# A fused attention and token-mixing kernel: the first four x tiles turned on TensorE in place of DMA transposes, with new engine orders

## The chip, the cores and the metric

The kernel runs on one core of a Trainium2 chip. The metric is device time in microseconds of one execution. The kernel before was timed three times: median 170.32 us, lowest 170.24, highest 170.61. One further execution was profiled; everything said about single instructions comes from that one.

## The reference, cut to what matters

```python
x = A_x                                        # (1, 2048, 448), bf16
g = sigmoid((x * gate_w).sum(-1, keepdims=True))
# A: 16 heads of 28, four segments of 512 rows
q, k, v = x @ wq, x @ wk, x @ wv               # split by head and segment
for s in range(4):
    a_dot = softmax(q_s @ k_s.T * 28**-0.5 + causal_mask) @ v_s
    a_mem = (phi(q_s) @ M) / (phi(q_s) @ z + 1e-6)
    o_s = sigmoid(beta) * a_mem + (1 - sigmoid(beta)) * a_dot
    M, z = M + phi(k_s).T @ v_s, z + phi(k_s).sum(rows)
a = concat(o) @ wo
# B: mixing over the 2048 rows (tokens), per column of x
h = layernorm(x)
u = gelu(h.T @ w1 + b1)                        # (448, 1792)
b = (u @ w2 + b2).T
out = g * a + (1 - g) * b
```

## The kernel before, in words

x has 2048 rows, held as 16 tiles of 128 rows. It is needed in two layouts. As rows (`xh`, one slot for each tile) it feeds the layer norm and then the first mixing product. Turned (`xT`, feature on the partition, the 448 features cut into four chunks c that start at 0, 128, 256 and 320) it feeds the projections to v, k and q. The kernel loads x twice: as rows by plain DMAs (`load_x`, names `ldx0`, `ldx4` and so on, after the first tile of each), and turned by DMA transposes (`transpose_x`, names `dtx{tc}_0` for chunks 0 to 2 and `dtx{tc}_1` for chunk 3, where tc counts groups of four tiles, 512 rows).

The program is a list of operations with names. Each states what it reads and writes, and the semaphore waits are worked out from that. The order on each engine is not decided by a scheduler at run time: it is written out in the table `ORDER`, one list of names for each of TensorE (PE), ScalarE (ACT), VectorE (DVE), GpSimd (POOL) and SyncE (SP). A number behind `@` is the PSUM bank that the operation takes, a number behind `*` a repeat.

Names that the rest of this document uses:

- `warm`, `warm2`: products of constants into bank 3 that nothing reads; `gtr`: a product that turns the gate weights, behind the load `ldgw`; `gw`: their copy by DVE into the weights of v.
- `pra{t}`, `prb{t}`, `lo{t}`, `prt{t}`: the v projection of tile t, by chunks 0, 1, the shared last 128 rows of the features, and the rest. `prk`, `prx`, `prq` with `lok`, `loq`: the same for k and q of a group and a set of heads.
- `ldwv*`, `ldwk*`, `ldwq*`: weight loads. ACT issues those of v and one of k, SP the others. `ldb1`, `ldb2`: biases, issued by ACT. `padk*`, `padx*`, `padq*`: copies by DVE that spread the weights of k and q to 32 columns for each head.
- `cpv`, `cpk`, `cpq`: copies from PSUM after a projection (ACT or DVE); `gt`: the gate's tanh on ACT; `ek`, `eq`: exponentials for phi.
- `bns`, `bna`, `ln`: layer norm statistics and application, on DVE. `sc`: scores; `exp`: softmax exponentials on ACT, 2048 columns each; `mask`: causal masks on POOL; `pv`: probabilities times v; `ot`: the turn of the attention output on DVE; `lw`, `wo`: output projection; `u`, `y`: the two mixing products; `ag`: gating of the attention output; `fin` and `out`: last mix and store.

TensorE runs products in several shapes: over the whole array, over two halves of its rows (`lo*`), over four strips of 32 rows (`sc`) or of 32 columns (`pv`, and `u`, `y` products that stand beside a `pv`). Products of one line (L296) appear for nearly all projections and mixing products, since one helper issues them.

The start of the program, in order: ACT issues the loads of the v weights and the gate weights; SP issues the DMA transposes of the first group (`dtx0_0`, `dtx0_1`), then the weights of k and q, then the transposes of the second group, then rows of x; TensorE runs nine `warm` products, `gtr`, `warm2`, and then the v projections of tiles 0 to 3. `early` projections (group 0) take banks 0 to 3 in turn.

The lines that the change touches: `transpose_x(0)` with the loads below it (from line 552), `warm_up` (line 660), the resources of `xT` (line 500: two for each group, chunks 0 to 2 and chunk 3), their use in `proj_d`, `do_k` and `do_v` (lines 761 to 870), and `ORDER` (line 318).

Of the kernel before, what the change touches and what calls it, by code (L numbers as in the profile page):

```python
# [324 lines left out]
u1-15 u2-10*4 u3-5*2 u4-0@4 u3-7*2 sc1_1 u5-0@6*2 u2-14 u5-2*2 u2-15 u3-9*6 u5-4 u3-15 u4-1*5 u5-5*2 pv1@7 u4-6*2
sc1_2 u4-8 u5-7*5 u4-9*4 u5-12 pv0@5 u5-13 sc1_3 u4-13*3 u6-0@7*3 u7-0@5 u6-3 u5-14 u6-4*2 u5-15 u6-6 sc1_4 u6-7 u7-1
u6-8*4 u7-2*2 u6-12 u7-4*3 u6-13*3 sc2_0 u7-7*7 pv2@6 u7-14*2 sc2_1 mst0@4 u8-0@6*2 prq2_1@7 prq2_0@5 loq2_0 sc2_2
u8-2*4 prq2_2@4 u8-6*4 prq2_2h@7 loq2_2 mem1 u8-10*2 u9-0@4 u8-12 u9-1*8 u8-13*2 u11-0@5 sc2_3 u9-9*3 pv3@7 u9-12
u8-15 u9-13*2 u11-1 u9-15 u11-2*4 sc2_4 u10-0@7*3 u11-6*6 u13-0@4 u10-3 pv4@6 sc3_0 u10-4*12 u11-12 u13-1 sc3_1
u13-2*3 u11-13*2 u13-5*2 pv5@6 u11-15 prt9@7 u13-7*4 sc3_2 lot8@6 u13-11*2 u12-0@5*5 prt8 u13-13*3 u12-5 sc3_3  # L330
lot10@67 u12-6*3 prt11 u12-9*7 prt10 sc3_4 mst1@7 prk3_1@4 pv6@5 prk3_0@7 lok3_0 sc4_0 prq3_1@6 prq3_0@7 wo0@5 loq3_0
lw0@4 sc4_1 wo1 pv7@6 prk3_2@5 wo3@7 lok3_2@4 lw2@6 sc4_2 wo2 prx3_3 y0-0@5*5 mem2 y0-5*9 prq3_2h@6 prq3_2@4 loq3_2
sc4_3 y1-0@7*7 y2-0@4 y1-7 y2-1 sc4_4 y2-2*2 y1-8 y3-0@6*3 pv8@5 y2-4 y1-9 sc5_0 y2-5*2 y3-3*3 y1-10 y3-6*5 sc5_1
y3-11*3 y1-11*3 y2-7 wo4@5 sc5_2 lw4@7 wo5 y2-8 pv9@6 y2-9*2 sc5_3 y2-11*3 y5-0@5*7 sc5_4 lw6@64 y5-7 pv10@7 wo7
y5-8*2 sc6_0 y4-0@7 y5-10*4 wo6 y4-1*2 sc6_1 pv11@4 y4-3*3 y6-0@6*2 mst2@5 sc6_2 y4-6 y6-2*5 prt13@4 lot12@5 mem3
y6-7*5 y4-7*2 prt12 y4-9*2 y6-12*2 sc6_3 lot14@45 prt15 prt14 y4-11*3 sc6_4 pv12@5 y7-0@4*3 wo9@7 lw8@5 sc7_0 wo8
y7-3*7 sc7_1 y7-10*2 pv13@6 y7-12*2 y8-0@5*4 sc7_2 y8-4*2 y9-0@7*3 y8-6 wo10@6 y8-7 sc7_3 wo11@4 y8-8*4 y9-3 y8-12*2
y9-4 sc7_4 lw10 y9-5*5 pv14@5 y10-0@6*7 y9-10*2 pv15@4 y11-0@5 y10-7 y11-1*3 y10-8*2 y9-12*2 y11-4*5 y10-10*2 y11-9*3
lw12 lw14 y10-12 y11-12*2 y10-13 wo14 wo15 wo12 y12-0@4*2 wo13 y13-0@7*4 y15-0@5 y13-4*2 y14-0@6*2 y13-6*4 y12-2
y14-2*2 y13-10 y14-4 y12-3*2 y13-11 y12-5*3 y14-5 y15-1 y12-8*3 y14-6*3 y13-12*2 y12-11*3 y14-9*5 y15-2*12 y15-0#1@7  # L340
y15-1#1 y15-2#1 y15-3#1 y15-4#1 y15-5#1 y15-6#1 y15-7#1 y15-8#1 y15-9#1 y15-10#1 y15-11#1 y15-12#1 y15-13#1""",
    "ACT": """
ldwv0 ldgw ldwv1 ldwv2 ldwvb ldwkb ldb1 ldb2 cpv2 cpv0 gt0 gt2 cpv1 gt3 gt1 ek0_0 cpk0_1 cpk0_3 cpq0_3 ek0_1 cpv7 gt7
cpk1_3 cpq1_3 cpk1_2 cpv6 cpq0_2 gt6 cpq0_0 cpq0_2#1 cpq1_1 cpq1_2 cpq0_1 tb eq1_1 cpq1_2#1 exp0_0@2 cpk1_1 cpv5 cpv4
gt5 gt4 exp0_1@3 cpk2_2 cpk2_3 cpk2_1 exp0_2@4 cpk2_0 exp0_3@0 eq1_0 eq1_2 exp0_4@1 ek0_2 gsq0 exp1_0@5 gsq1 gvh1 gth0
exp1_1@6 gsq2 gth1 ek0_3 eq1_3 gsq3 gvh3 exp1_2@0 ek1_0 gth3 gth2 exp1_3@1 gsq4 gsq5 exp1_4@2 ek1_1 gth5 gth4 exp2_0@3
gsq6 gsq7 exp2_1@4 ek1_2 cpq2_1 exp2_2@5 ek1_3 cpq2_0 gth7 cpq2_2#1 gth6 eq2_2 eq2_0 exp2_3@6 gsq8 gsq9 eq2_1 gvh9
exp2_4@0 gth8 gth9 exp3_0@1 ek2_0 gsq10 ek2_1 gvh10 exp3_1@2 gsq11 gth10 exp3_2@3 cpv9 cpv8 gt8 gt9 gth11 exp3_3@4
cpv11 gsq13 gt11 gsq12 cpv10 exp3_4@0 gth12 gt10 cpk3_0 exp4_0@5 eq2_3 cpq3_1 cpq3_0 exp4_1@6 gth13 cpk3_2 exp4_2@7
cpk3_3 ag2 eq3_1 cpq3_3 ag3 ek2_2 exp4_3@1 ek2_3 exp4_4@2 eq3_0 exp5_0@0 eq3_2 exp5_1@3 exp5_2@4 exp5_3@5 ag5 exp5_4@6  # L350
eq3_3 exp6_0@1 ag6 exp6_1@2 exp6_2@7 cpv13 gt13 cpv12 gt12 exp6_3@0 gt15 gt14 exp6_4@3 exp7_0@4 ag9 exp7_1@5 exp7_2@6
exp7_3@1 exp7_4@2 ag11 ag15 ag14 ag12 ag13""",
# [1026 lines left out]
```

## Time and profile before

| what | value |
|---|---|
| time, median of three runs | 170.32 us (170.24 to 170.61) |
| time of the profiled execution | 170.1 us |
| its span, first to last instruction | 168.3 us |
| instructions | 4931 |
| DMA | 25.44 MB in 53974 packets, mean 151 GB/s |
| HBM read, written | 18.82 MB, 2.36 MB |
| DVE, ACT, POOL busy | 81%, 77%, 38% |

How to read the views: the page gives each engine's busy time. The chain of waits follows back from the last instruction to whatever released it, step by step, so it says which engine or DMA the end hangs on. The timeline lists instructions by start, with equal ones merged and a count behind x; in brackets stands the idle time of the engine before and what ended it. "PEld" is TensorE's weight load, which overlaps the product before it. A name with q behind the engine (ACTq, SPq) is the engine's sequencer, which issues DMAs. Windows give busy time by stretch. A matmul's listed duration includes its way through the array; products that follow each other start closer together than that.

The DMA share of the first slices of the span is high: by fortieths of the span (4.2 us each) it reads 6, 9, 9, 9 tenths, and the moved bytes 144, 259, 225 and 296 GB/s.

### The profile page before, as it was taken

What the parts mean: (1) busy time and instruction counts of PE and PEld (TensorE: products, weight loads), DVE (VectorE), ACT (ScalarE), POOL (GpSimd) and SP (SyncE); (2) the same over time, 40 slices, a digit from 0 to 9 for tenths busy, and PEclk for the clock granted to TensorE, in tenths of its full rate; (3) what the DMA queues carried; (4) which work ended last, traced back from release to release, by engine and by line L of the source; (5) the groups of instructions that cost most, each with busy time, mean ns of one, the idle gap of its engine ahead of it and who ended that gap; (6) DMA issues with size and microseconds to landing.
All of it is one profiled execution on the core that took longest, in us unless ns stands there. A gap on an engine that the chain in (4) does not pass through costs nothing.

```text
span 168.3 us, 4931 instructions
## 1 busy us (share of the span) xinstructions
PE 164.0 (97%) x2017; PEld 77.6 (46%) x2017; DVE 136.9 (81%) x321; ACT 130.4 (77%) x164; POOL 64.5 (38%) x100
## 2 busy tenths in 40 slices
PE   8799999999999999999999999999999999999994
PEld 3234444444554544544453454444454444454553
DVE  0087999877989989999999999999999979695042
ACT  0359999999999997999999998988985798603200
POOL 5000245261442514142177356445838356541000
DMA  6999999886677955994338202328942129730302
GB/s 144 259 225 296 242 236 237 167 220 189 181 158 221 217 101 146 163 213 126 103 108 182 67 2 63 97 77 157 253 126 84 42 63 283 225 117 27 117 27 82
DMA packets 53974, 25.44 MB, mean 151 GB/s; under 512 B 18416, under 2 KB 53712, under 8 KB 53952
## 3 DMA queue, kind: packets, MB, share of 16 engines
q1 hardware_dynamic: 53160, 24.54, 59.2%
q10 hardware_dynamic: 792, 0.58, 1.6%
q8 instruction: 16, 0.26, 0.7%
q14 instruction: 6, 0.05, 0.1%
HBM read 18.82 MB, written 2.36 MB: 126 GB/s over the span
## 4 chain that ended last, share of the span: by engine, by line
PE 94%; DMA 3%; ACTq 1%; POOL 0%; issue 0%; DVE 0%; POOLq 0%
PE t L296 79%; PE t L1015 8%; PE t L1045 5%; DMA t<-in_A_wv_dram 3%; PE t L896 1%; PE t L1118 1%; ACTq L538 1%; ACTq L559 0%; DVE t L1251 0%; POOL t L557 0%; POOL t L633 0%; POOL t L600 0%; PE t L927 0%; POOL t L632 0%; POOL t L628 0%
## 5 line engine op out<-in xcount | busy, mean ns | idle before, releaser
L296 PE MATMUL t<-t 128*32 128x448 bf16 (+8 forms) x1252 | 140.5, 352 | 1.1 <-DMA t<-in_A_wv_dram 1.0
L296 PEld LDWEIGHTS t<-t 128*32 128x32 bf16 (+2 forms) x1252 | 63.0, 97 | 64.3 <-issue 14.2
L1024 ACT ACTIVATE t<-t 128x2048 bf16<-128x2048 f32 x40 | 75.2, 1879 | 6.8 <-PE t L1015 6.2
L1027 POOL TENSOR_SCALAR_AFFINE_SELECT t<-t 128x512 bf16<-128x512 bf16 x64 | 43.5, 691 | 42.5 <-ACT t L1024 39.6
L1082 POOL TENSOR_TENSOR t<-t 128x448 bf16<-128x448 f32 (+2 forms) x13 | 13.3, 1026 | 19.0 <-DVE t L1075 14.4
L1251 DVE SCALAR_TENSOR_TENSOR t<-t 128x448 bf16<-128x448 f32 (+2 forms) x17 | 10.7, 645 | 10.2 <-PE t L296 10.1
L1015 PE MATMUL t<-t 28*128 28x512 bf16 (+3 forms) x256 | 15.8, 301 | 0.0
L1059 DVE STREAM_TRANSPOSE t<-t 128x512 f32<-128x512 f32 x16 | 11.3, 706 | 2.9 <-PE t L1045 2.7
L965 POOL TENSOR_TENSOR t<-t 128x4 f32<-128x4 f32 x4 | 4.2, 1054 | 23.3 <-DVE t L963 21.6
L1157 ACT ACTIVATE t<-t 128x448 bf16<-128x448 f32 x10 | 7.0, 732 | 7.7 <-PE t L296 7.7
L1045 PE MATMUL t<-t 128*32 128x512 bf16 (+3 forms) x256 | 11.5, 299 | 0.0
L1101 DVE STREAM_TRANSPOSE t<-t 128x512 bf16<-128x512 bf16 x16 | 10.9, 690 | 0.0
L1015 PEld LDWEIGHTS t<-t 28*128 28x128 bf16 x256 | 4.4, 92 | 14.0 <-ACT t L1024 7.7
L956 DVE BATCH_NORM_STATS2 t<-t 128x6 f32<-128x448 bf16 x16 | 9.3, 610 | 1.1 <-DMA t<-in_A_x_dram 1.1
L857 ACT ACTIVATE t<-t 128x448 bf16<-128x448 f32 x13 | 6.8, 546 | 4.2 <-PE t L296 4.2
L1220 DVE SCALAR_TENSOR_TENSOR t<-t 128x448 f32<-128x448 f32 x14 | 9.2, 664 | 0.5 <-ACT t L1215 0.4
L1045 PEld LDWEIGHTS t<-t 128*32 128x32 bf16 x256 | 6.7, 97 | 5.3 <-issue 0.4
L1212 ACT ACTIVATE t<-t 128x448 f32<-128x448 f32 x14 | 8.8, 638 | 0.1
L818 ACT ACTIVATE t<-t 128x512 bf16<-128x512 bf16 x12 | 7.6, 635 | 1.4 <-DVE t L775 1.4
L847 DVE SCALAR_TENSOR_TENSOR t<-t 128x512 bf16<-128x512 bf16 x12 | 8.5, 712 | 0.1
L1075 DVE SCALAR_TENSOR_TENSOR t<-t 128x448 f32<-128x448 f32 x12 | 8.4, 698 | 0.0
L1225 DVE SCALAR_TENSOR_TENSOR t<-t 128x448 bf16<-128x448 f32 x14 | 8.4, 614 | 0.0
(76 smaller groups left out, 129.3 us busy)
## 6 DMA issues: line engine op xcount, KB each, us to landing
t<-in_B_w_dram SPq DMA_DIRECT2D x52, 256.0 KB, 3.4
t<-in_A_x_dram SPq DMA_DIRECT2D x4, 448.0 KB, 4.8
out_dram<-t SPq DMA_DIRECT2D x15, 112.0 KB, 1.9
t<-in_B_w_dram SPq DMA_DIRECT2D x8, 128.0 KB, 2.4
t<-in_A_wv_dram ACTq DMA_DIRECT2D x4, 112.0 KB, 4.1
t<-in_A_wq_dram SPq DMA_DIRECT2D x1, 336.0 KB, 5.1
spare_heads<-t SPq DMA_DIRECT2D x8, 32.0 KB
spare_heads<-t SPq DMA_DIRECT2D x16, 16.0 KB
```

The costliest lines, as they stand in the source:

```text
L296: last = e.matmul(out[q], w[:, q], x, skip_group_check=True, **kw)
L956: op("DVE", lambda e: e.bn_stats(st6[:, t, :], xh[:, t, :]), reads=[R_x[t]], writes=[R_st6[t]], name=f"bns{t}", cost=512, prio=P_PROJ - 10 ...
L1015: last = e.matmul(bank(hl)[:, c0 : c0 + w], kT[r, hg, s * 512 + j * 128 : s * 512 + j * 128 + 128], qT[r, hg, s * 512 + 128 * j : s * 512 ...
L1024: exps.append(op("ACT", lambda e: e.activation(pslot(g), ps[:, 0:4, :], ACT.Exp, scale=SCALE), reads=R_bank[0:4], writes=[g.res], take=g, ...
L1027: op("POOL", lambda e, c0=c0: e.affine_select(pslot(g)[:, :, c0 : c0 + 128], pslot(g)[:, :, c0 : c0 + 128], pattern=[[0, 4], [1, 128]], co ...
L1045: last = e.matmul(bank(cb)[32 * ((hl + hg) % 4) : 32 * ((hl + hg) % 4) + 32, 128 * j : 512], vaug[:, 4 * s + j, 32 * h : 32 * h + 32], psl ...
L1059: dv(lambda e: e.transpose(tt[:, ia, :], bank(cb)[:, 0:512]), [bres(cb)], [R_tt[ia]], "ta", 630, use=(cb,))
L1082: return e.tensor_tensor(dst, part(n3[0]), part(n3[1]), op=ALU.add)
L1101: dv(lambda e: e.transpose(oT[:, hg, s * 512 : s * 512 + 512], o), [R_ob[hg]] + ([R_obx] if hg else []), qres(hg, s), "ot", 635)
L1212: op("ACT", lambda e: e.activation(gg[:, q, :], bank(b)[:, 0:D], ACT.Square, bias=b1s[:, ft : ft + 1], scale=math.sqrt(GC)), **buse(b), re ...
L1220: op("DVE", lambda e: e.scalar_tensor_tensor(gg[:, q, :], gg[:, q, :], 1.0, vh[:, q, :], op0=ALU.add, op1=ALU.mult), reads=[R_gg[q], R_vh[ ...
L1251: op("DVE", lambda e: e.scalar_tensor_tensor(outst[:, p, c0:c1], bank(b)[:, 0 : c1 - c0], omg[:, T : T + 1], ag(T)[:, c0:c1], op0=ALU.mult ...
```

## The change

The first four tiles of x are no longer read by DMA transposes. Their rows, which the kernel loads in any case, are loaded first of all on SP, in two DMAs of two tiles each (`ldx0`, `ldx2`) in place of the one of four tiles (`ldx0`) that stood behind the second group's transposes. TensorE multiplies each tile's chunk by the identity: four operations `xt{p}_{k}` for the tile pairs p = 0, 1 and the chunk pairs k = 0, 1, four products of 128 columns each, into PSUM bank 2p + k. Four copies `cx{p}_{k}` of 512 columns bring them to `xT`; the table puts `cx0_0`, `cx1_0` and `cx1_1` on ACT and `cx0_1` on DVE. `xT` of group 0 has four resources, one for each pair of pairs, so that a v projection of tiles 0 and 1 on chunks 0 and 1 waits for `cx0_0` alone. The groups 1 to 3 keep their DMA transposes. The leading `warm` has five products and not nine. All five orders are written anew; the total of the other products stays the same, though some stand in other shapes (tiles 8 to 9 and 12 to 13 of v, and parts of `u12`, `y6`, run as halves of the rows).

The core of the diff:

```diff
     "PE": """
-warm gtr@4 warm2 pra0@5 pra1@6 pra2@7 pra3@4 prb3 prb2 prb0 prb1 lot2 lot0 prt1 prt3 prt2 prt0 pra0_1 pra0_2 pra0_0
+warm gtr@4 warm2 xt0_0 xt0_1 xt1_0 pra0@5 xt1_1 pra1@6 pra3@7 prb3 prb1 pra0_1 pra2@4 pra0_2 pra0_0 prb2 prb0 lot0
...
     "ACT": """
-ldwv0 ldgw ldwv1 ldwv2 ldwvb ldwkb ldb1 ldb2 cpv2 cpv0 gt0 gt2 cpv1 gt3 gt1 ek0_0 cpk0_1 cpk0_3 cpq0_3 ek0_1 cpv7 gt7
+ldwv0 ldgw ldwv1 ldwv2 ldwvb ldwkb cx0_0 cx1_0 cx1_1 ldb2 cpv1 cpv3 gt3 cpv2 gt0 gt1 cpk0_1 cpk0_3 gt2 cpq0_3 ek0_1
+ek0_0 cpv7 cpk1_3 gt7 tb cpk1_2 cpq0_2 cpq1_3 cpv6 cpq0_1 gt6 ldb1 cpq0_0 cpq1_2 cpq1_2#1 exp0_0@2 cpk1_1 cpk1_0 cpv4
...
     "DVE": """
-ob0 gw padk0 padx0 cpv3 padk1 padx1 padk2 padx2 padq0 padq1 b2c padq2 b1c padq3 cpk0_0 cpk0_2 mk0_0 bns3 bns1 bns0
+bns1 ob0 bns0 gw bns3 cx0_1 bna3 padx0 padk0 padx2 padq0 padq2 padx1 bna1 padk1 padk2 padq1 cpv0 bns2 cpk0_0 padq3
...
     "SP": """
-dtx0_0 dtx0_1 ldwk0@0 ldwk1 ldwq0@1 ldwqb dtx1_0 dtx1_1 ldx0 ldx4 ldx8 ldbeta ldw1_0_0 dtx2_0 ldx12 dtx2_1 ldw1_0_1
+ldx0 ldx2 ldwk0@0 ldwk1 ldwq0@1 ldwqb dtx1_0 dtx1_1 ldx4 ldx8 ldbeta ldw1_0_0 dtx2_0 ldx12 dtx2_1 ldw1_0_1 ldw1_1_0
...
-    R_xT = [R(f"xT{t}_", 2) for t in range(4)]
+    R_xT = [R(f"xT{t}_", 4 if t == 0 else 2) for t in range(4)]
+
+    def xres(tc, cs=range(NCT), halves=range(2)):
+        return [R_xT[0][k] for k in sorted({2 * p + c // 2 for p in halves for c in cs})] if tc == 0 else \
+            [R_xT[tc][k] for k in sorted({c // 3 for c in cs})]
...
-    transpose_x(0)
+    load_x("SP", 0, 2)
+    load_x("SP", 2, 2)
...
-    load_x("SP", 0, 4)
...
-    warm_up(9, "warm", -1)
+    def turn_x():
+        for p in range(2):
+            for k in range(2):
+                b = 2 * p + k
+
+                def fn(e, p=p, k=k, b=b):
+                    for c in (2 * k, 2 * k + 1):
+                        for t in range(2):
+                            at = 256 * (c % 2) + 128 * t
+                            last = e.matmul(bank(b)[:, at : at + 128], xh[:, 2 * p + t, C0[c] : C0[c] + 128], ident[:, :],
+                                            start=True, stop=True, skip_group_check=True)
+                    return last
+
+                op("PE", fn, reads=R_x[2 * p : 2 * p + 2] + [R_ident], writes=[R_bank[b]], name=f"xt{p}_{k}", mode="f",
+                   cost=pe_cost(128, 128, 128, 128), prio=-1)
+
+                def ends(p=p, k=k, b=b):
+                    return (xT[:, 2 * k : 2 * k + 2, 256 * p : 256 * p + 256],
+                            bank(b).rearrange("p (c t) -> p c t", c=2))
+
+                op("ACT", lambda e, ends=ends: e.activation(*ends(), ACT.Copy), reads=[R_bank[b]], writes=[R_xT[0][b]],
+                   name=f"cx{p}_{k}", cost=act_cost(512), prio=-1,
+                   alt=("DVE", lambda e, ends=ends: e.tensor_copy(*ends()), dve_cost(512)))
+
+    warm_up(5, "warm", -1)
     warm_up(1, "warm2", P_PROJ + 0.01, 3500.0)
+    turn_x()
...
-        rx = R_xT[t // 4]
+        def rx(cs=range(NCT)):
+            return xres(t // 4, cs, (t % 4 // 2,))
```

The three places that matter below are the starts of TensorE, ACT and SP. On TensorE, before, from the first product (x9 counts equal products in a row; 128x512 by the constant is `warm`, 128x3 and 128x1 are `gtr`, 128x449 are v projections, 128x512 k projections):

```order
L664 MATMUL t<-const-bfloat16-1.0 128x512 x9
L879 MATMUL t<-t 128x3
L880 MATMUL t<-t 128x1
L664 MATMUL t<-const-bfloat16-1.0 128x512
L296 MATMUL t<-t 128x449 x16
L296 MATMUL t<-t 128x512 x6
```

The same place after the change (the 128x128 products of L697 are `xt`):

```order
L682 MATMUL t<-const-bfloat16-1.0 128x512 x5
L924 MATMUL t<-t 128x3
L925 MATMUL t<-t 128x1
L682 MATMUL t<-const-bfloat16-1.0 128x512
L697 MATMUL t<-t 128x128 x12
L296 MATMUL t<-t 128x449
L697 MATMUL t<-t 128x128 x4
L296 MATMUL t<-t 128x449 x4
L296 MATMUL t<-t 128x512 x2
```

Twelve products by the identity now stand ahead of the first v projection, four behind it, and four constant products are gone.

On ACT, before, from its first instruction to its first copies from PSUM (in_B_b is the biases, the table load comes with the first activation of the program, 128x16x28 is `cpv`):

```order
L538 DMA t<-in_A_wv_dram 128x448
L559 DMA t<-in_gate_w_dram 6x128
L538 DMA t<-in_A_wv_dram 128x448 x2
L542 DMA t<-in_A_wv_dram 128x448
L542 DMA t<-in_A_wk_dram 128x448
L568 DMA t<-in_B_b_dram 14x128
L570 DMA t<-in_B_b_dram 16x128
L857 ACT_TABLE_LOAD
L857 ACTIVATE t<-t 128x16x28 x2
```

And after (128x2x256 is `cx`):

```order
L556 DMA t<-in_A_wv_dram 128x448
L578 DMA t<-in_gate_w_dram 6x128
L556 DMA t<-in_A_wv_dram 128x448 x2
L560 DMA t<-in_A_wv_dram 128x448
L560 DMA t<-in_A_wk_dram 128x448
L708 ACT_TABLE_LOAD
L708 ACTIVATE t<-t 128x2x256 x3
L588 DMA t<-in_B_b_dram 16x128
L900 ACTIVATE t<-t 128x16x28 x2
```

The table load moved ahead of the two bias issues and now stands right before the copies of the turned tiles; the second bias issue moved to a place between the tanh `gt6` and the copy `cpq0_0`.

On SP, before, its first issues:

```order
L548 DMA_TRANSPOSE t<-in_A_x_dram 128x3x512
L548 DMA_TRANSPOSE t<-in_A_x_dram 128x1x512
L538 DMA t<-in_A_wk_dram 128x2x448
L538 DMA t<-in_A_wk_dram 128x448
L538 DMA t<-in_A_wq_dram 128x3x448
L542 DMA t<-in_A_wq_dram 128x448
L548 DMA_TRANSPOSE t<-in_A_x_dram 128x3x512
L548 DMA_TRANSPOSE t<-in_A_x_dram 128x1x512
L533 DMA t<-in_A_x_dram 128x4x448 x3
```

And after:

```order
L551 DMA t<-in_A_x_dram 128x2x448 x2
L556 DMA t<-in_A_wk_dram 128x2x448
L556 DMA t<-in_A_wk_dram 128x448
L556 DMA t<-in_A_wq_dram 128x3x448
L560 DMA t<-in_A_wq_dram 128x448
L566 DMA_TRANSPOSE t<-in_A_x_dram 128x3x512
L566 DMA_TRANSPOSE t<-in_A_x_dram 128x1x512
L551 DMA t<-in_A_x_dram 128x4x448 x2
```

Two transposes at the head gave way to two plain loads, and one plain load of four tiles behind the second group's transposes is gone.

More of the change, by code (lines that the diff above doesn't have):

```diff
@@ L325 @@
[L325 to L339, printed above, removed]
@@ L346 @@
[L346 to L350, printed above, removed]
@@ L762, in proj_d @@
         ts = slice(tc * 512 + t0, tc * 512 + t0 + n)
-        need = R_xT[tc]
+        need = xres(tc)
         return dict(n=n, w=lambda c, rows: wqk[rows, c, 4 * G : 4 * G + 4, :].rearrange("p h j -> p (h j)"),
                     x=lambda c, rows: xT[rows, c, ts], need=need + R_w, use=xuse(tc).get("use", ()),
-                    by=lambda c: [need[c // 3]] + [R_w[k] for k in range(len(R_w)) if R_w[k] not in R_wkp or k % 3 == (0, 0, 1, 2)[c]],
+                    by=lambda c: xres(tc, (c,)) + [R_w[k] for k in range(len(R_w)) if R_w[k] not in R_wkp or k % 3 == (0, 0, 1, 2)[c]],
                     name=name + ("h" if t0 else ""), out=out)
@@ L778, in do_k @@
         if tc == 0:
-            P["first"] = [((0, 1), [R_xT[0][0], R_wkp[0], R_wkp[3]])]
+            P["first"] = [((0, 1), xres(0, (0, 1)) + [R_wkp[0], R_wkp[3]])]
         return P
```

121 lines of the change are left out of this document (77 added, 44 removed).

## The prediction

> **What bounds the kernel now.** First the page's busy times and the windows, then the chain, then the start in the timeline. In the windows the columns are start:end, length, and busy time of each engine with its instructions.
>
> ```profile
> PE 164.0 (97%) x2017; PEld 77.6 (46%) x2017; DVE 136.9 (81%) x321; ACT 130.4 (77%) x164; POOL 64.5 (38%) x100
> ```
> ```profile
> 4.59:7.43 2.84, 1.86 (x9) 0.63 (x9) 0.00 (x0) 1.28 (x1) 0.00 (x0) 1.00 1.15 238
> 7.43:20.00 12.57, 12.57 (x74) 5.48 (x75) 9.95 (x32) 9.61 (x25) 0.54 (x1) 1.00 1.06 258
> 20.00:166.00 146.00, 145.94 (x1925) 70.14 (x1923) 126.17 (x288) 119.50 (x139) 61.74 (x85) 1.00 0.57 142
> ```
> ```profile
> PE t L296 <- DMA t<-in_A_wv_dram: 0.6, 1, 0.6
> ```
>
> TensorE is busy in every part of 7.43 to 20 and in all but 0.06 us of 20 to 166. The third fence lists the waits of TensorE's products from 7.43 on: one, of 0.6 us, and it is the one that ends at 7.43. So from 7.43 on TensorE sets the time by itself. Only two things can move it: how early this full stream starts, and what is in it.
>
> The chain, in its own words (start, length, what):
>
> ```profile
> 2.93 4.36 DMA t<-in_A_wv_dram
> 7.43 2.78 PE t L296 x14
> ...
> 20.80 0.33 PE t L1015 x4
> ...
> 30.19 2.38 PE t L296 x12
> ```
>
> Before 7.43 the end hangs on the last v weights, issued at 2.93, landed 4.36 us later. TensorE's start, with the waits in brackets:
>
> ```profile
> 0.82 3.38 PE L664 MATMUL t<-const-bfloat16-1.0 128*128 128x512 bf16 x9 [0.82 <-PEq L1364]
> 4.09 0.38 PE L664 MATMUL t<-const-bfloat16-1.0 128*128 128x512 bf16 x1
> 4.59 0.92 PE L296 MATMUL t<-t 128*128 128x449 bf16 x4
> 5.91 0.93 PE L296 MATMUL t<-t 128*128 128x449 bf16 x4 [0.40 <-DMA t<-in_A_wv_dram]
> 7.43 2.78 PE L296 MATMUL t<-t 64*128 64x449 bf16 x14 [0.59 <-DMA t<-in_A_wv_dram]
> ```
>
> Eight v products run between 4.59 and 7.43. The chain's 12 products of 448 columns in 2.38 us make 0.19 each (a change of array shape at their end taken off), so eight make 1.5. Had they run without a pause up to 7.43 they would have begun at 7.43 - 1.5 = **5.9**. That is the number to beat: the start that counts.
>
> **The change, part by part.** Durations are from the profiled execution: 168.3 us of span, 170.1 in time, 0.2 below the median of 170.32. I work out a difference against the profiled execution and add it to the median.
>
> *Loads.* ACT's and SP's first issues, q marking the sequencer:
>
> ```profile
> 0.78 0.38 ACTq L538 DMA_DIRECT2D t<-in_A_wv_dram  x1
> 1.20 0.73 ACTq L559 DMA_DIRECT2D t<-in_gate_w_dram  x1
> ...
> 3.57 0.64 ACTq L542 DMA_DIRECT2D t<-in_A_wk_dram  x1
> 4.24 0.45 ACTq L568 DMA_DIRECT2D t<-in_B_b_dram  x1
> 4.71 0.37 ACTq L570 DMA_DIRECT2D t<-in_B_b_dram  x1
> 5.12 1.28 ACT L857 ACT_TABLE_LOAD   x1 [5.12 <-issue]
> 8.70 0.98 ACT L857 ACTIVATE t<-t 128x448 bf16<-128x448 f32 x2 [2.30 <-PE t L296]
> ```
> ```profile
> 0.79 2.67 SPq L548 DMA_TRANSPOSE t<-in_A_x_dram  x2
> 3.51 1.08 SPq L538 DMA_DIRECT2D t<-in_A_wk_dram  x2
> ```
>
> Two transposes occupy SP for 2.67 us. Two plain loads cost about 0.55 each (the two of wk: 1.08), so every later issue on SP comes some 1.6 us earlier, and a 448 KB load of rows further back is gone. This takes the load wait away: the weights of v, which ended the chain's DMA piece, no longer share the engines with transposes. What is late next?
>
> *ACT's table load.* It stands behind ACT's DMA issues and starts as the last one ends (4.71 + 0.37, then 5.12). Before, it had 2.3 us to spare: the first copy waited for TensorE until 8.70. Now the first copy, `cx0_0`, stands right behind it, and the first v product waits for that copy. The two bias issues ahead of it moved away, 5.12 - 4.24 = 0.88, so the load starts at 4.24 and ends at 5.52. The copies' prices:
>
> ```profile
> L773 ACT ACTIVATE t<-t x8: 581/598/633, 12.6 to 95.8; 128x512 bf16<-128x512 f32 x8
> L775 DVE CAST t<-t x4: 652/674/692, 11.3 to 90.7; 128x512 bf16<-128x512 f32 x4
> ```
>
> `cx0_0` takes 0.60, to 6.12, and with a hand-over of under 0.1 the first v product starts at **6.2**, where it was 4.59. `cx1_0` ends at 6.72, just as two v products and `xt1_1` have passed and `pra3` asks for it (6.8). `cx1_1` and, on DVE, `cx0_1` (0.67) are asked for only by the k products and `lot0`, over 1 us later. These copies, 2.5 us in all, lie in time in which both engines sat idle.
>
> The bounds of 6.2: ACT's issues took 0.37 to 0.73. At 0.37 each the six ahead of the table load end near 3.2, the load near 4.5, and the identity products decide instead (next). At 0.7 each they end near 5.1, the copy at 7.0. I take 6.2, since these are the same six instructions and the rows show their places.
>
> *Identity products.* Sixteen of 128 columns.
>
> ```profile
> L296 PE MATMUL t<-t 128*128 128x128 bf16 x14 | 0.9, 219 | 0.0
> ```
>
> Fourteen of this size occupy 0.9 us, 0.06 each. Twelve stand ahead of the first v product. They wait for x: the first plain load of the trace (v weights) landed 2.1 us after its issue, rows of x behind other traffic 4.0 to 5.4:
>
> ```profile
> DMA to landing us min/median/max: 2.1/4.4/5.1
> ```
> ```profile
> DMA to landing us min/median/max: 4.0/4.8/5.4
> ```
>
> So the first tiles land between 2.9 and 4.8, with `xt0_0` done by about 4.6, at worst 5.2: hidden behind the table load either way. Four products (`xt1_1`) stand between v products and cost 4 x 0.06 = 0.2. The four lost `warm` products cost nothing in themselves; they ran while loads were under way.
>
> [...]
>
> *The stream.* Counted by columns and array shape, all other products are the same work in both orders (more halves of rows, fewer strips of columns). A change of array shape costs about 0.11: four scores of 512 columns side by side take 0.33 in the chain, and one pass of 512 columns is 0.22 (12 of 448 give 0.19). I count 112 changes from the first v product on before, 110 now: **-0.2**.
>
> *Tail.* Before:
>
> ```profile
> 162.77 3.92 SPq L1255 DMA_DIRECT2D out_dram<-t  x5
> 163.57 0.68 DVE L1251 SCALAR_TENSOR_TENSOR t<-t 128x448 bf16<-128x448 f32 x1 [0.24 <-PE t L296]
> 165.20 0.55 DVE L1251 SCALAR_TENSOR_TENSOR t<-t 128x320 bf16<-128x320 f32 x1 [0.95 <-PE t L296]
> 165.98 0.35 DVE L1251 SCALAR_TENSOR_TENSOR t<-t 128x128 bf16<-128x128 f32 x1 [0.23 <-PE t L296]
> ```
>
> The new order ends with the last of tile 14, then 12 products of 128 columns, 0.7 us. Tile 14's mix (0.68) therefore ends just as the last piece may start; before it was over 1.7 us earlier. **+0.05**, and its store may hold SP for 0.3 in front of the last one.
>
> *Sum.* The start that counts: 6.2 + 0.2 (`xt1_1`) = 6.4 against 5.9, +0.5; changes of shape -0.2; tail +0.05. Two short waits of the old start, behind the weights' spreading copies, should go with the earlier loads: -0.2. Together **+0.1**: 170.2 for an execution like the profiled one, **170.4** against the median. This kernel's runs can tell some 0.2% (0.34 us) from no change, so the forecast is "no difference": one wait takes the place of another.
>
> **The rivals.**
>
> *Even (0.42).* As summed: 170.1 to 170.6.
>
> *Faster: the table load comes early (0.25).* If ACT's issues go at the 0.38 of the first one, the table load is over by 4.5 and `cx0_0` waits for `xt0_0` alone: 4.7 + 0.6, first v product at 5.4, 0.8 earlier: **169.6**. For it: the slow issues of the rows (0.6) fell while SP issued transposes. Against: the 0.64 of wk fell while SP issued plain loads, as it will now.
>
> *Slower: the clock (0.17).* TensorE's weight loads in the warm-up show its pace:
>
> ```profile
> 2.06 0.15 PEld L664 LDWEIGHTS t<-const-bfloat16-1.0 128*128 128x128 bf16 x1 [0.28 <-issue]
> 2.48 0.15 PEld L664 LDWEIGHTS t<-const-bfloat16-1.0 128*128 128x128 bf16 x1 [0.28 <-issue]
> ```
>
> 0.42 to 0.43 us for 512 columns, twice the 0.22 of later. Nine took 3.38, less than 9 x 0.43 = 3.9, so full pace came near 3.4, after 2.6 us of work. Five will stop near 2.9, after 2.1 us, and a pause follows until the gate weights land. If that isn't enough and 2.6 us must be worked anew, the slow pace lasts from 6.2 to between 7.1 (the products ahead of 6.2 counted) and 8.8 (not counted), and half of that time is lost: 0.45 to 1.3, **170.9 to 171.7**. It decides from a threshold between 2.1 and 2.6 us of work. The granted clock of the windows reads 1.00 throughout and doesn't show this.
>
> [...]
>
> *Slower: the moved bias issue (0.16).* ACT's row before the first scores, and TensorE's behind it:
>
> ```profile
> 20.66 0.38 ACT L835 ACTIVATE t<-t 128x256 bf16<-128x256 f32 x1
> 21.06 0.58 PE L296 MATMUL t<-t 64*128 64x512 bf16 x4
> ```
>
> The copy of q ends at 21.04 and frees the bank in which TensorE goes on at 21.06: no slack. `ldb1` (0.45) now stands on ACT right ahead of the last copies of q, so the first scores and the shared k products behind them can be that late, and all of TensorE with them: up to 0.45, **170.9**. It decides once ACT has less than 0.45 us of idle time between its first copies and this place.
>
> That the load change does nothing (x lands no earlier than the transposes, 4.59) would still be hidden: the copy waits for the table load until 5.52.
>
> **How the numbers follow.** The likeliest is 170.4. The first rival's 169.6 and its spread give the low end, 169.4. The clock rival's middle gives the high end, 171.5; the rest of it, and an order that stalls elsewhere, I leave out at under 2 in 10. Faster by over 0.2% is the first rival: 0.25. Within 0.2%: 0.42. Slower: 0.17 + 0.16 = 0.33.
>
> **What would show it.** The table load near 4.2 and no idle time between it and the first 128x512 copy; the first product of 449 columns near 6.2, its wait ended by ACT; no wait for the v weights. A first v product before 5.7 shows the faster case. Products 0.37 apart behind 6.2 show the slow clock. Idle time of TensorE's products before the first scores, near 20, ended by ACT, shows the bias issue. The prediction is wrong altogether if TensorE waits for long behind 25, where the orders are new but the work isn't.

## The result, and the profile after

| | before | after |
|---|---|---|
| time, median | 170.31 us (170.24 to 170.61) | 176.99 us (176.42 to 177.29) |
| profiled execution, its span | 170.1, 168.3 us | 176.42, 174.4 us |
| DVE, ACT, POOL busy | 136.9, 130.4, 64.5 us | 151.2, 128.4, 61.6 us |

After to before: 1.0385, 95% interval 1.0354 to 1.0416. The change costs 6.7 us; the forecast was no difference. The page's busy times and its chain by engine:

```profile
PE 165.3 (95%) x2005; PEld 78.6 (45%) x2010; DVE 151.2 (87%) x340; ACT 128.4 (74%) x159; POOL 61.6 (35%) x90
PE 64%; DVE 27%; DMA 3%; ACT 2%; issue 1%; SPq 1%; POOL 0%; ACTq 0%; POOLq 0%
```

TensorE's busy time is 1.3 us longer, VectorE's 14.3 us. The chain, which was TensorE for 94% of the old span, runs through VectorE for 27%. The windows (start:end, length, then TensorE, its weight loads, VectorE, ScalarE, GpSimd) show where:

```profile
8.00:20.00 12.00, 11.95 (x71) 5.43 (x70) 9.44 (x34) 8.16 (x23) 1.03 (x1) 1.00 1.16 227
...
49.00:70.00 21.00, 20.13 (x329) 9.88 (x327) 20.41 (x44) 19.68 (x25) 6.65 (x9) 1.00 0.89 200
70.00:93.00 23.00, 21.65 (x330) 10.21 (x332) 22.93 (x45) 20.18 (x28) 8.96 (x10) 1.00 0.36 92
93.00:108.00 15.00, 14.17 (x155) 6.33 (x149) 15.00 (x31) 13.88 (x20) 7.78 (x10) 1.00 0.40 86
```

From 49 to 108 VectorE is busy for 58.34 of 59 us and TensorE idle for 3.05. In the same windows of the kernel before, VectorE was busy for 56.29 us, so already 95%, and TensorE throughout:

```profile
49.00:70.00 21.00, 21.00 (x339) 10.32 (x341) 20.18 (x45) 20.08 (x26) 6.82 (x12) 1.00 0.77 172
70.00:93.00 23.00, 23.00 (x351) 10.97 (x347) 21.87 (x48) 22.56 (x31) 10.34 (x13) 1.00 0.61 150
93.00:108.00 15.00, 15.00 (x189) 7.06 (x182) 14.24 (x34) 14.35 (x17) 7.24 (x10) 1.00 0.20 55
```

Its total of 81% hid this: of its 31 us of idle time, 7.0 lay in the first 7.4 us and 13.0 in the last 28. What TensorE's products wait for (line, releaser: sum, times, longest):

```profile
PE t L924 <- DMA t<-in_gate_w_dram: 1.0, 1, 1.0
PE t L296 <- DVE t L1263: 0.7, 2, 0.4
PE t L296 <- DVE t L1206: 0.7, 1, 0.7
PE t L941 <- ACT t L903: 0.6, 1, 0.6
PE t L1060 <- DVE t L1171: 0.6, 1, 0.6
PE t L296 <- DMA t<-t: 0.6, 1, 0.6
...
```

No single wait is over 0.7 behind the start, and GpSimd ends none of them. Of some 4.4 us in all, 2.9 are a PSUM bank (or an operand) that a late instruction of VectorE releases; the DMA one is a store of a turned output (`go3_0`) that itself waited for VectorE and for a weight load on SP. One of them, the scores at 68.32, with VectorE ahead of it:

```profile
61.89 0.72 DVE L959 TENSOR_TENSOR t<-t 128x128 bf16<-128x128 f32 x1
62.53 0.60 DVE L1025 TENSOR_SCALAR t<-t 128x4 f32<-128x4 f32 x1
63.04 0.70 DVE L1146 STREAM_TRANSPOSE t<-t 128x512 bf16<-128x512 bf16 x1
63.67 0.65 DVE L876 CAST t<-t 128x512 bf16<-128x512 f32 x1
64.24 0.63 DVE L1265 SCALAR_TENSOR_TENSOR t<-t 128x448 f32<-128x448 f32 x1
64.80 1.05 DVE L1134 SCALAR_TENSOR_TENSOR t<-t 128x448 bf16<-128x448 f32 x1
65.77 2.50 DVE L1171 STREAM_TRANSPOSE t<-t 128x512 f32<-128x512 f32 x4
```
```profile
68.32 0.40 PE L1060 MATMUL t<-t 28*128 28x512 bf16 x4 [0.57 <-DVE t L1171]
```

VectorE runs without a pause into the four transposes (`tm`) that empty the banks of the scores. Look at the lengths: a product of 128x128 lasts 0.72, a scaling of 128x4 (512 numbers) 0.60. That is the thread that the experiments end at. The start:

```profile
4.15 0.19 PE L924 MATMUL t<-t 128*128 128x3 bf16 x1 [1.03 <-DMA t<-in_gate_w_dram]
4.61 1.49 PE L697 MATMUL t<-t 128*128 128x128 bf16 x12
5.93 0.56 PE L296 MATMUL t<-t 128*128 128x449 bf16 x1
6.28 0.63 PE L697 MATMUL t<-t 128*128 128x128 bf16 x4
6.71 1.75 PE L296 MATMUL t<-t 128*128 128x449 bf16 x5
```
```profile
3.71 1.28 ACT L708 ACT_TABLE_LOAD   x1 [3.71 <-issue]
5.28 0.60 ACT L708 ACTIVATE t<-t 128x512 bf16<-128x512 f32 x1 [0.29 <-PE t L697]
```

Twelve identity products take 1.3 us and products of 449 columns are some 0.37 apart, against 0.19 in `e4` below: TensorE runs at half pace until about 8 us. The table load is over at 4.99, and the first copy waits for TensorE.

What the new table does to engines, besides order: of the operations that both kernels have, ten went from GpSimd to VectorE (`ox0 oy0 oy4 o5 ox8 o9 ox12 oy12 o14 o15`, sums of attention and memory, `ox0` and `oy0` plain copies), seventeen from ScalarE to VectorE (`cpv0 cpv5 gvh1 gvh3 ag3` and others), nine back.

### The profile page after: what moved, and what is told of

Read it like the earlier page. It is cut to its first block, busy times and chain, and to the rows that moved or that the text cites. A ratio compares the mean times of both kernels' runs of the same rounds, so it can differ in the third digit from the quotient of the medians.

```text
span 174.4 us, 4926 instructions
## 1 busy us (share of the span) xinstructions
PE 165.3 (95%) x2005; PEld 78.6 (45%) x2010; DVE 151.2 (87%) x340; ACT 128.4 (74%) x159; POOL 61.6 (35%) x90
## 4 chain that ended last, share of the span: by engine, by line
PE 64%; DVE 27%; DMA 3%; ACT 2%; issue 1%; SPq 1%; POOL 0%; ACTq 0%; POOLq 0%
PE t L296 54%; PE t L1060 5%; PE t L1090 3%; DVE t L1104 3%; DVE t L1270 2%; DVE t L1263 2%; DVE t L1265 2%; DVE t L1120 2%; DVE t L1122 2%; DVE t L1146 2%; DMA t<-in_gate_w_dram 2%; DMA t<-t 2%; DVE t L1171 1%; DVE t L865 1%; DVE t L1134 1%; DVE t L1206 1%
## 5 line engine op out<-in xcount | busy, mean ns | idle before, releaser
L296 PE MATMUL t<-t 128*32 128x448 bf16 (+11 forms) x1228 | 140.6, 352 | 3.2 <-DVE t L1263 0.7
L1072 POOL TENSOR_SCALAR_AFFINE_SELECT t<-t 128x512 bf16<-128x512 bf16 x64 | 49.6, 795 | 64.8 <-ACT t L1069 64.0
L1202 ACT ACTIVATE t<-t 128x448 bf16<-128x448 f32 x6 | 4.3, 724 | 15.9 <-PE t L296 15.8
L1206 DVE TENSOR_SCALAR t<-t 128x448 bf16<-128x448 f32 x10 | 7.3, 734 | 3.8 <-PE t L296 3.8
L1263 DVE TENSOR_SCALAR t<-t 128x448 f32<-128x448 f32 x11 | 7.3, 674 | 3.2 <-ACT t L1257 3.2
L1127 POOL TENSOR_TENSOR t<-t 128x448 bf16<-128x448 f32 (+1 forms) x5 | 5.4, 1087 | 12.7 <-DVE t L1120 6.4
L900 ACT ACTIVATE t<-t 128x448 bf16<-128x448 f32 x11 | 5.9, 544 | 4.8 <-PE t L296 4.8
L1270 DVE SCALAR_TENSOR_TENSOR t<-t 128x448 bf16<-128x448 f32 x14 | 9.1, 669 | 0.3 <-ACT t L1268 0.3
L865 DVE SCALAR_TENSOR_TENSOR t<-t 128x512 bf16<-128x512 bf16 x12 | 9.0, 748 | 0.0
L1120 DVE SCALAR_TENSOR_TENSOR t<-t 128x448 f32<-128x448 f32 x12 | 8.9, 742 | 0.1
```

The lines of the kernel that those rows point to most:

```text
L296: last = e.matmul(out[q], w[:, q], x, skip_group_check=True, **kw)
L865: op("DVE", lambda e: e.scalar_tensor_tensor(kphi[:, p, :], ks, 0.0, kphi[:, p, :], op0=ALU.max, op1=ALU.add), reads=kres(hg, tc) + [R_kph ...
L1072: op("POOL", lambda e, c0=c0: e.affine_select(pslot(g)[:, :, c0 : c0 + 128], pslot(g)[:, :, c0 : c0 + 128], pattern=[[0, 4], [1, 128]], co ...
L1120: dv(lambda e: e.scalar_tensor_tensor(n3[0], n3[0], oc, rb[0], op0=ALU.mult, op1=ALU.mult), [R_tt[ia], R_rec[tb], R_omcol], [R_tt[ia]], "o ...
L1263: alt=("DVE", lambda e: e.tensor_scalar(vh[:, q, :], bank(b)[:, 0:D], 0.5, b1h[:, ft : ft + 1], op0=ALU.mult, op1=ALU.add), dve_cost(448)))
L1270: op("DVE", lambda e: e.scalar_tensor_tensor(uT[:, ft, :], gg[:, q, :], 1.0, vh[:, q, :], op0=ALU.add, op1=ALU.mult), reads=[R_gg[q], R_vh ...
```

## The experiments

In the diffs of `ORDER`, which are cut to what moves, each line is a piece of one engine's list; "after" and "before" name the kernel that the edit starts from. Each ratio is to the kernel before, timed beside it.

### The start and the old orders

`e3_start_alone`, from before's table with after's code:

```diff
-warm gtr@4 warm2 pra0@5 pra1@6 pra2@7 pra3@4
+warm gtr@4 warm2 xt0_0 xt0_1 xt1_0 pra0@5 xt1_1 pra1@6 pra2@7 pra3@4
-ldwkb ldb1 ldb2 cpv2
+ldwkb cx0_0 cx1_0 cx1_1 ldb1 ldb2 cpv2
-ob0 gw padk0
+ob0 gw cx0_1 padk0
-dtx0_0 dtx0_1 ldwk0@0
+ldx0 ldx2 ldwk0@0
```

> The new start (two row loads, sixteen identity products, four copies, five warm-ups) in front of the old orders of all five engines. Theory (the start costs what TensorE shows behind the first scores, 5.0 us late after against 3.9 before): 171.2 to 171.8. Rival (the start costs nothing, as I predicted, and everything is lost later): 170.0 to 170.6. Rival (a late start also upsets what follows): over 173.

Measured 171.76 us (171.3 to 171.94), 1.0074 [1.0047, 1.0102]: the start costs 1.4 us, and what follows is not upset. In its trace nothing but loads and start-up holds TensorE:

```profile
PE t L911 <- DMA t<-in_gate_w_dram: 1.1, 1, 1.1
...
PE t L959 <- DMA t<-in_B_b_dram: 0.4, 1, 0.4
```

So the other 5 us belong to the new orders.

`e5_before_pool_to_dve`, from before, the ten sums and copies moved (two of them shown):

```diff
-garg5 garg4 mk1_1 rec1 phk1_1
+garg5 garg4 ox0 mk1_1 rec1 oy0 phk1_1
...
-mask1_0_0 oy0 ox0 mask2_0_0
+mask1_0_0 mask2_0_0
```

> The kernel before, with the ten adds and copies put on VectorE at about the places that the new table gives them; nothing else changed. Theory (VectorE has no room at these places): 172 to 174.5, TensorE's waits ending at VectorE. Rival (31 us of VectorE's time were idle before, the 6 us fit in there): 170.2 to 170.8.

173.4 us, 1.0175 [1.0144, 1.0206]. TensorE now waits for VectorE three times, of which the two longest:

```profile
PE t L296 <- DVE t L1060: 0.9, 1, 0.9
...
PE t L1046 <- DVE t L1162: 0.8, 1, 0.8
```

`e9_before_copies`, from before, the other 26 moves alone, each by its start time.

> The kernel before, with the other 26 moves alone (seventeen copies and gatings from ScalarE to VectorE, nine back), each at the place in the other queue that its start time in the old trace gives; the ten stay on GpSimd. About 6 us more work on VectorE net. Theory (VectorE has no room): 172 to 174, as with the ten (173.4). Rival (these fit, only the ten do harm): 170.2 to 171.

173.65 us, 1.0202 [1.0175, 1.0229]. In the old orders there was room for neither: 3.0 and 3.5 us. With the start that makes 7.9, more than the 6.7 lost. It looked settled: VectorE has too much to do. But `e9`'s trace has 1.5 us of TensorE's waits ending at ScalarE and 1.1 at VectorE, so the places in the queues count too, and the tests in the changed kernel itself say otherwise.

### Taking the operations back

`e1b_pool_back`, from after, the ten back in GpSimd's list at the places that they had in the old one; `e2b_most_back`, with eleven of the other moves undone as well. All 36 at once were not measured: `e2_all_back`, and a first version of the ten (`e1_pool_back`), gave no result.

> The changed kernel with the ten adds and copies that the new table moved from GpSimd to VectorE (ox0, oy0, oy4, o5, ox8, o9, ox12, oy12, o14, o15) back on GpSimd; all else as changed. Theory (VectorE is overloaded; the ten alone cost the old kernel 3.0 us in the run before this): busy time of VectorE near 145, 2 to 3.5 of the 6.7 us come back, 173.5 to 175. Rival (the new orders of TensorE and SP make the waits, VectorE is only what comes last): 176 to 177.3.

> As the kernel beside it, and eleven more operations back: gvh1, gvh3, cpv11, cpk3_3, ag3, ag5, ag6, ag12 from VectorE to ScalarE, gvh5, cpq3_2 and its second half from ScalarE to VectorE. Theory: busy time of VectorE near 142, a further 1 to 1.5 us comes back, 172 to 174. Rival (the ten on GpSimd were all of it, ScalarE has as little room): the same as the kernel beside it within 0.4 us, or slower.

179.48 us (1.0532 [1.0481, 1.0583]) and 181.87 us (1.0664 [1.0634, 1.0693]): slower than after by 2.5, outside both forecasts, and by 4.9, where only the rival's "or slower" fits. The waits of `e1b_pool_back` tell why:

```profile
PE t L1090 <- POOL t L1072: 4.7, 3, 2.5
```

GpSimd takes its list in order, and masks that `pv` needs stood behind sums that weren't ready: the sum at 124.11 had waited 2.27 us for VectorE, and the masks behind it came at 125.19. A bad place, so neither run tests the theory (`e2b_most_back` has 3.0 us of such waits). `e8_pool_back_late` puts each of the ten behind the masks that had started by the time at which VectorE did it:

```diff
-mask1_0_0 mask2_1_1
+mask1_0_0 ox0 oy0 mask2_1_1
...
-mask3_0_0 ox4 mask3_4_1 mask3_3_0 mask3_4_3 o6
+mask3_0_0 oy4 ox4 mask3_4_1 mask3_3_0 mask3_4_3 o5 o6
```

> The ten adds and copies back on GpSimd once more, each now placed behind the masks that had started on GpSimd when VectorE did it in the changed kernel, so that no mask stands behind an add that isn't ready. Theory (the ten on VectorE cost 2 to 3.5 us, and the run before lost because masks stood behind adds): no waits of TensorE for masks over 0.5 us, 173.5 to 175. Rival (GpSimd is no better place in this order whatever the position, since an add takes twice as long there and holds the turn behind it): 176.5 or more.

176.74 us, 1.0375 [1.0334, 1.0416]: nothing gained, though one wait of 0.6 us for a mask is left. `e10_small_adds` leaves the ten where they are and makes them small:

```diff
+                    if small:
+                        return e.tensor_tensor(dst[..., 0:1], part(n3[0])[..., 0:1], part(n3[1])[..., 0:1], op=ALU.add)
                     return e.tensor_tensor(dst, part(n3[0]), part(n3[1]), op=ALU.add)
```

> The changed kernel, the same operations on the same engines in the same order, but the ten adds and copies treat only the first column of each block (of 12, 16 or 28), so most of their sums are left out; ob0 clears all of ob ahead of everything else on VectorE. Some 4 us of VectorE's work are gone and no order changed. Theory (VectorE's total work sets the pace behind 49 us): 2 to 3.5 us faster, 173.5 to 175. Rival (waits on VectorE come from where operations stand in its queue, behind something late, not from how much there is): 176 to 177.

175.78 us, 1.0327 [1.0287, 1.0367]: about 1 us of the 2 to 3.5 expected, though VectorE's busy time also fell by only 1.6 us (the longer `ob0` counted). The theory in its simple form, too many operations, has little support in the changed kernel. But the test was weaker than I thought: of the ten only `oy4` and `o5` stand between 61 and 98 us, where VectorE is full.

### The place in the queue

`e12_after_dve_order`, from after, only VectorE's list:

```diff
-mstc0 omg0 ot1 cpq2_0 garg6 oa2 tm4 tm6 tm5 tm7
+mstc0 ot1 cpq2_0 garg6 oa2 tm4 tm6 tm5 tm7 omg0
-phk1_2 gvh8
+gvh8 phk1_2
-gelu10 oy4 ot3 gelu11 cpv11
+gelu10 gelu11 cpv11 oy4 ot3
-cpk3_3 phq2_3 ag3
+cpk3_3 ag3 phq2_3
-ta9 b2g2 rec9 oa9 ag5
+ta9 ag5 b2g2 rec9 oa9
-o13 fin10
+fin10 o13
```

> The changed kernel with seven places of VectorE's own order mended and nothing else: omg0 behind tm7, gvh8 ahead of phk1_2, gelu11 and cpv11 ahead of oy4 and ot3, ag3 ahead of phq2_3, ag5 right behind ta9, fin10 ahead of o13. No operation changes its engine, so VectorE has the same work. Theory (each wait of TensorE behind 49 us is one operation that frees a bank and stands in VectorE's queue behind work that nobody waits for; taking work off elsewhere didn't help because the queue fills up anew from one product to the next): the waits at 68 (0.64), 73 (0.5), 90 to 93 (0.7, 0.25, 0.6), 103 (0.72), 123 (0.3) and 156 (0.7) go or halve, 173 to 174.5. Rival (VectorE's total work is the bound; what is moved back only shifts the wait to the next place): 176.2 to 177.2.

176.6 us, 1.0367 [1.0329, 1.0404]: the rival's time. Waits that were aimed at went, and others came:

```profile
PE t L296 <- DVE t L1263: 1.0, 1, 1.0
...
PE t L1060 <- DVE t L1025: 0.6, 1, 0.6
PE t L296 <- DVE t L1104: 0.5, 1, 0.5
PE t L1060 <- ACT t L1069: 0.5, 1, 0.5
```

Mending seven places doesn't make VectorE less late. And the wait at 68 stayed, for a plain reason: `omg0` (0.60 in after, L1025 above) was taken out of the way, and `garg6`, which lasted 0.63 there (L1265 at 64.24), now lasts 1.09. Extra length had moved from one instruction to another:

```profile
63.98 1.09 DVE L1265 SCALAR_TENSOR_TENSOR t<-t 128x448 f32<-128x448 f32 x1
```

With that I read lengths and not counts.

### Turns with GpSimd

From the trace of after, VectorE and GpSimd (POOL) beside each other:

```profile
83.81 2.02 DVE L1122 TENSOR_TENSOR t<-t 128x448 f32<-128x448 f32 x2
85.75 1.05 DVE L1120 SCALAR_TENSOR_TENSOR t<-t 128x448 f32<-128x448 f32 x1
86.72 1.05 DVE L1270 SCALAR_TENSOR_TENSOR t<-t 128x448 bf16<-128x448 f32 x1
```
```profile
83.70 3.60 POOL L1072 TENSOR_SCALAR_AFFINE_SELECT t<-t 128x512 bf16<-128x512 bf16 x4 [2.19 <-ACT t L1069]
```

Four instructions of VectorE of about 1.0 each lie beside four masks of 0.7 to 1.02. The shorter ones of the same forms last 0.58 to 0.67, and such a mask 0.64. Where they meet both are longer, as if each waited for the other in turn; that is my reading of the rows, and such pairs are called turns below. I took for every form of instruction (line, operation, shape) the length that a fifth of its instructions stay under, and added up what lies over it by more than 0.15 us. After: 24 long instructions on VectorE, 9.7 us in sum, 12 of them (5.1 us) between 49 and 108 us. Before: 7, 2.3 us, and none between 49 and 108. Every one of them lies beside an instruction of GpSimd, which by the same count has 23 long ones, 9.6 us (before: 12, 4.3 us). On VectorE that is 7.4 of the 14.3 us by which its busy time grew.

The same count fits the runs so far. `e8`, `e10` and `e12` have 24, 23 and 26 long instructions on VectorE (9.7, 9.3 and 10.1 us), and all three stay within 1.2 us of after; even `e2b_most_back`, with 21 of the 36 operations back, has 20 (8.4 us). The moves put into the old orders make few: 11 (4.4 us) in `e5`, and 7 (2.7 us) in `e9`, whose loss of 3.5 us is therefore hardly theirs. So the turns come with the new orders far more than with the operations that changed engines; which part of the orders brings them about was not tested.

To take the turns away with the same operations, engines and orders, `e14_narrow_masks` narrows the masks; `e15_before_narrow_masks` does the same to the kernel before, `e16_narrow_masks_pool_back` to `e8`, `e17_repaired_narrow_masks` to `e13` (below):

```diff
-            op("POOL", lambda e, c0=c0: e.affine_select(pslot(g)[:, :, c0 : c0 + 128], pslot(g)[:, :, c0 : c0 + 128],
-                                                        pattern=[[0, 4], [1, 128]], compare_op=ALU.is_ge, fill=0.0,
+            op("POOL", lambda e, c0=c0: e.affine_select(pslot(g)[:, :, c0 : c0 + 8], pslot(g)[:, :, c0 : c0 + 8],
+                                                        pattern=[[0, 4], [1, 8]], compare_op=ALU.is_ge, fill=0.0,
```

> The changed kernel with every causal mask on GpSimd narrowed from 128 to 8 columns of each block (the rest of the diagonal blocks stays unmasked), so GpSimd's masks take some 0.2 us and not 0.64; same operations, engines and orders. In the changed kernel's trace some two dozen instructions of VectorE last 0.4 us longer than others of their kind, 9.7 us in sum (before: seven, 2.3 us), and each of them lies beside a mask that is longer too. Theory (VectorE, full from 49 to 108 us, loses these 7 us by taking turns with GpSimd, and TensorE waits for it): the long instructions fall below 4 us in sum, VectorE's busy time falls by 5 or more, time 171.5 to 174. Rival (the moved operations alone fill VectorE, the long ones fall in its idle time): 176 to 177.

> The kernel before with the same narrowed masks (the rest of the diagonal blocks stays unmasked). TensorE sets its time and waits for no mask, so by either theory 169.9 to 170.6. If it came out much faster, narrowing would help by itself and the kernel beside it would show nothing.

`e14`: 172.48 us (171.46 to 173.71), 1.0125 [1.0072, 1.0178], 4.5 us less than the changed kernel. The control: 170.37 us, 0.9994 [0.9979, 1.0009], no change. The same place of `e14`, and all that the view of waits lists for TensorE:

```profile
82.49 1.21 DVE L1122 TENSOR_TENSOR t<-t 128x448 f32<-128x448 f32 x2
83.63 0.67 DVE L1120 SCALAR_TENSOR_TENSOR t<-t 128x448 f32<-128x448 f32 x1
84.23 0.62 DVE L1270 SCALAR_TENSOR_TENSOR t<-t 128x448 bf16<-128x448 f32 x1
```
```profile
82.47 1.92 POOL L1072 TENSOR_SCALAR_AFFINE_SELECT t<-t 128x32 bf16<-128x32 bf16 x4 [2.65 <-ACT t L1069]
```
```profile
PE t L924 <- DMA t<-in_gate_w_dram: 1.3, 1, 1.3
PE t L682 <- PEq L1409: 0.8, 1, 0.8
```

The four instructions that took from 83.81 to 87.77 now take from 82.49 to 84.85, and the four masks beside them 1.92 and not 3.60. No long instruction is left on VectorE, its busy time is 142.6 us, and TensorE waits for nothing behind the start, with all 36 moved operations still on their new engines. (The profiled execution is the fastest of `e14`'s four, 171.46; the others have no profile.)

A rival is that shorter masks help because what follows them starts earlier. It has no support: in after's view of waits neither TensorE, VectorE nor ScalarE waits for GpSimd, and its chain is GpSimd's for 0%.

> Narrowed masks (as above), and the ten adds and copies back on GpSimd behind the masks. With full masks moving the ten back brought nothing (176.7). Theory (there it only exchanged work of VectorE for longer turns; with short masks the work taken away counts): 1 to 2 us faster than narrowed masks alone. Rival (the ten never mattered in this order): the same within 0.4.

173.0 us, 1.0146 [1.0103, 1.0189], against 172.48: no gain. The difference of 0.5 is a little over the rival's 0.4, but inside the intervals. In the new order taking the ten off VectorE doesn't help, with full masks or with narrow ones.

### The clock at the start

`e4_start_warm9`, from `e3`, and `e11_after_warm9`, from after, have the old nine warm-ups:

```diff
-    warm_up(5, "warm", -1)
+    warm_up(9, "warm", -1)
```

> The new start in front of the old orders (171.8 before), with nine warm-ups in place of five, so that TensorE is busy until the gate weights land at 4.1. Theory (five warm-ups leave the slow clock on: identity products and the first v products at half pace until about 8 us): identity products near 0.06 apart, products of 449 columns 0.19 apart from the first on, time 170.3 to 171.0. Rival (the warm-ups don't matter, the waits for copies and x do): 171.5 to 172.

> The changed kernel with nine warm-ups in place of five. With the old orders this brought 1.0 us (171.8 to 170.8). Theory (the start's loss adds to the later waits): 175.7 to 176.3. Rival (behind 49 us VectorE sets the pace and takes the gain back as longer waits): 176.6 to 177.3.

170.75 us (1.0029 [1.0013, 1.0045]) against 171.76, and 175.7 us (1.0316 [1.0262, 1.0369]) against 176.99: about 1.0 and 1.3. The start of `e4`:

```profile
4.57 0.83 PE L684 MATMUL t<-t 128*128 128x128 bf16 x12
5.65 0.36 PE L296 MATMUL t<-t 128*128 128x449 bf16 x1 [0.25 <-ACT t L695]
5.85 0.39 PE L684 MATMUL t<-t 128*128 128x128 bf16 x4
6.07 1.50 PE L296 MATMUL t<-t 128*128 128x449 bf16 x7
7.95 2.29 PE L296 MATMUL t<-t 64*128 64x449 bf16 x12 [0.39 <-DMA t<-in_A_wv_dram]
```

Four identity products pass in 0.2 and products of 449 columns stand 0.19 apart. With five warm-ups (`e3`) sixteen identity products stand 0.107 apart, and full pace comes only at 7.1. The v weights are late again, at 7.95; half pace had hidden it. `e11` is less clear: in its profiled execution, the slowest of its four (176.56), nearly all of the first twelve identity products still stood 0.107 apart, and full pace came near 6.3.

`e7_start_warm9_bias`: from `e4`, with `ldb2` and `ldb1` issued by SP behind `ldwqb`.

> As the kernel beside it, and the two bias loads issued by SP behind the weights of q, no longer by ScalarE behind the copies. Theory (in the new start with the old orders the bias product waits 0.4 us for its load, which ScalarE issues only at 7): 0.3 to 0.5 faster than the kernel beside it, 169.9 to 170.6. Rival (another load is late next, or the second group's transposes behind them on SP come 0.9 later and stop the v products of tile 7): no faster.

170.75 us, 1.0027 [1.0012, 1.0042]: no faster, though no wait for the bias is left in its trace. Its profiled execution reached full pace only near 5.4 us, that of `e4` near 3.8 (below), so the two traces don't show what took the gain.

### Together

`e13_after_repaired`: `e12` with nine warm-ups, the spreading copies of k ahead of those of q on VectorE, `go3_0` ahead of `ldw2_7_1` on SP, `u7-10` two products later.

> As the kernel beside it, with nine warm-ups, the weights of k spread before those of q, the store of one turned output (go3_0) ahead of a weight load on SP, and u7-10 two products later on TensorE. Theory (the start's clock is worth 1.0, the waits at 10, 50 and 159 together 1.1): 171 to 172.5. Rival (gains at the start are taken back behind 49 us by VectorE): within 0.7 of the kernel beside it.

> The changed kernel with nine warm-ups, VectorE's order mended at eight places, a store and one product moved (174.5 with full masks), and the masks narrowed as above. Theory (start, place in the queue and turns with GpSimd together are the whole loss): 170 to 171.3. Rival (something else in the new orders of TensorE and SP is left): over 172.

`e13`: 174.51 us, 1.0268 [1.0231, 1.0304], 2.1 less than `e12` and so between theory and rival. `e17`: 172.01 us, 1.0091 [1.0058, 1.0124], over the 171.3 that I had as the upper end and, barely, where the rival has it; in its trace 0.6 us of waits for weights of the mixing products are left. Against `e14` it is only 0.5 faster, within the intervals, so the parts don't simply add. No version with the new start beat the kernel before; the closest are `e4` and `e7`, 0.3% behind.

Of the 6.7 us, then: about 1.4 are the start (`e3`), 1.0 of it the half pace; about 4.5 are turns with GpSimd (`e14`). The rest, 0.8, is within the intervals of the runs that it is the difference of, and the split takes the parts to add.

## Why the prediction was wrong

**The step that failed** is the one headed "The stream": "Counted by columns and array shape, all other products are the same work in both orders", hence -0.2. The count holds: with each product weighed by the share of the array that it takes, warm-ups and identity products among them, before's trace and that of `e14`, whose order on TensorE is after's, both add up to 350,283 columns, with 112 and 110 changes of shape. What fails is that only TensorE was counted. It followed from "from 7.43 on TensorE sets the time by itself", which was true of the old orders alone: VectorE stood at 95% from 49 to 108 us with not one long instruction there. The new table puts 27 operations on VectorE and takes nine away, and the windows show what room it had. Neither was put into the sum. And even that count would have missed the larger part, since 142.6 us of VectorE's work do fit in the new orders (`e14`), while 142.3 and 142.4 us cost the old ones 3.0 and 3.5 (`e5`, `e9`): here most of the price, about 4.5 of 6.7 us, is set by what stands beside what on VectorE and GpSimd. The terms of the sum make +0.15, put down as +0.1, which changes nothing. The list of signs did name the place: "if TensorE waits for long behind 25".

**The table load** came at 3.71, not 4.24: ACT's six issues took 0.42 to 0.58 each and not the 0.38 to 0.73 of before. It ended at 4.99, between the 5.52 of the sum and the 4.5 of the "faster" rival, and half of that rival came true: the copy waited for `xt0_0` alone.

**Identity products** cost 0.107 each and not 0.06, twelve of them 1.3 us. The row that I took their price from ran at full pace. So the first v product came at 5.93, near the 6.2 forecast, by another way: that it is near is luck.

**The clock** was a rival at 0.17. The half pace that it forecast came at the start, at 1.0 us in `e4` and 1.3 in `e11`, within the 0.45 to 1.3 that it was given. That a slower clock makes it was not shown: from 4 to 8 us, where after's products are 0.37 apart, the granted clock reads 1.00. Its condition, a threshold between 2.1 and 2.6 us of work, does not hold: in `e5`, `e7` and `e11` TensorE worked without a pause from 0.83 to 4.6 and was still at half pace, where before was at full pace from about 3.4. More warm-ups helped on the whole, but no amount of work comes out of these traces.

**The moved bias issue** did not decide: TensorE's products end at 20.64 and the first scores start at 20.79.

**Waits for spreading copies** (-0.2) are gone, as forecast: TensorE is idle for 0.05 us between 8 and 20. **The tail** is 0.2 and not 0.05 longer: 2.6 us from TensorE's last product to the end, 2.35 before.

## What to carry to other kernels

When an order is written anew, put the work of every engine, stage by stage, beside the room that it had there; a total of 81% can be 95% in the stage that counts. Where VectorE and GpSimd both work on SBUF, look at the lengths of single instructions against others of the same form: here those that were 0.4 us longer lay beside one of the other engine, they counted as busy, and moving operations back or mending the order left about as many. To tell amount from contention, shrink the other engine's instructions and change nothing else, with the same edit on the old kernel as a control.
